# Linear attention gated by a mixer block: scale chains on GpSimd, a fixed turn for the first loads, key-value matrix times WO from rounded parts, and a new order

## The chip, the core and the metric

The kernel runs on one core of one Trainium2 chip. Its engines are TensorE (PE, with its weight loads PEld), VectorE (DVE), ScalarE (ACT), GpSimd (POOL) and SyncE (SP, which here only issues transfers). The metric is device time in microseconds of one execution; lower is better. Times of before: 502.96 us median of 3 runs (502.81, 502.96, 505.84).

## What is computed

x has 2048 rows (tokens) of 512 columns, in fp32. Both branches work on its layer norm; one is linear attention with 32 heads of 16, the other a spatial-shift mixer with an MLP, whose SiLU gates the first.

```python
def _A_ref(x, wqkv, wo):
    # q, k, v from x @ wqkv, 32 heads
    phi = lambda t: jnp.where(t > 0, t + 1, jnp.exp(t)) + 1e-6
    pq, pk = phi(q), phi(k)
    kv = jnp.einsum("bhsd,bhse->bhde", pk, v)
    z = jnp.einsum("bhsd->bhd", pk)
    num = jnp.einsum("bhqd,bhde->bhqe", pq, kv)
    den = jnp.einsum("bhqd,bhd->bhq", pq, z)[..., None] + 1e-6
    return (heads joined of num / den) @ wo

def _B_ref(x, w1, w2, w3, w4):
    h = _gelu(_layernorm(x) @ w1)
    hs = (quarters of h shifted by +1, -1, +2, -2 rows) @ w2
    x1 = x + hs
    return x1 + _gelu(_layernorm(x1) @ w3) @ w4

xn = _layernorm(x)
s = _A_ref(xn, A_wqkv, A_wo)
g = _silu(_B_ref(xn, B_w1, B_w2, B_w3, B_w4))
return x + s * g
```

## The kernel before

The rows are tiled by 128 into 16 tiles, and by four tiles into four blocks (QT = 4). The kernel doesn't issue its instructions where they are written: every helper (`mm`, `act`, `tt`, `ts`, `load`, `store`, `gather` and others) records an operation with what it reads and writes, and `emit` at the end chooses the order of each engine's row. It takes, again and again, the operation that can start first by estimated durations, and among those that can start at about the same time the one with the earliest due time (`op.due`). `deadlines` works the due times out backward from the order in which TensorE's products are written, and `nudged` then shifts single ones by a table of pairs (operation number, steps of a quarter microsecond). That table is SOONER, some 700 pairs. The order is fixed when the program is built; on the chip each engine works through its row and waits on semaphores.

Products of fp32 values are made in one of two ways. `mm(..., slow=True)` multiplies fp32 operands as they are. `products` multiplies values split into a rounded part (fp32r, names ending in h) and a rest (names ending in l): high times high, high times low, low times high, three fp32r products in place of one. `rounded` makes such a pair: ScalarE rounds, VectorE subtracts.

The stages around the change, in the order of time:

- **Start.** SP issues the loads of WK (four chunks wk_s0 to wk_s3, the first in two halves), of block 0 of transposed x (four chunks xt0_0 to xt0_3, each in two halves of 256 columns, since load_u is called with two parts), then of x and WQ. The first products are k0 and k1 from the unrounded first chunks (`raw_k`), then k2 and k3 from the rounded first chunk, then chunk 1 (wk_1h, u0_1h, u0_1l, wk_1l) and so on. At most eight transfers of SP are under way; the ninth waits for the first.
- **Scales.** For each tile the mean and variance of x are taken (`load_rows`). `scale_x` turns them into factors by a chain of small steps on 128 x 1 to 128 x 4 values: w (variance plus epsilon), rs (power of -0.5, on GpSimd), ns (minus rs), nm (mean times ns), mr or a second nm. `spread` makes a similar chain (pu, power, means) whose rows go through memory (arow, nrow) and come back as broadcast rows: `load_u` adds nrow to block b's xt by an accumulating load from GpSimd's queue (`gather`). `mixed` has a chain w2 for the second layer norm. In before, w, ns, pu and w2 stand on VectorE, all other steps on GpSimd.
- **Key-value matrix.** G gathers the product of x and the features of k. Four fp32 products per quarter (kv, with WV) and a mask give kvt, 128 x 512. Its four quarters times the chunks of WO give m, which ScalarE copies into the matrices mq for the attention.
- **Late stages.** Blocks 1 to 3 make the MLP's hidden values first and the down products at the end (`down_forms`, `down_late`), the last of them for block 1, whose hidden values were spilled to memory (hd) and are fetched back.

The lines that the prediction's steps touch are scale_x, spread and mixed (the small steps), the stage of kvt and m, and the call of emit with its table.

Of the kernel before, what the change touches and what calls it, by code (L numbers as in the profile page):

```python
# [11 lines left out]
ALU = mybir.AluOpType  # L12
# [68 lines left out]
class Op:  # L81
    __slots__ = ("eng", "busy", "lat", "emit", "pre", "post", "tiles", "opens", "two", "table", "patience", "soon", "loads",
                 "nom", "due", "ready", "at", "end", "mb", "order")


class Plan:
# [9 lines left out]
    def add(self, eng, busy, lat, reads, writes, emit, two=False, table=None, mb=0.0):  # L96
# [3 lines left out]
        op.order = len(self.ops)  # L100
# [142 lines left out]
    def deadlines(self, first):  # L243
        t = first
        for op in self.ops:
            if op.eng == "PE":
                op.nom = t
                t += op.busy
        for op in self.ops:
            op.due = op.nom if op.eng == "PE" else INF  # L250
        self.backward()
        for op in self.ops:
            op.at = max([p.at + p.lat for p in op.pre], default=0.0)
            if op.eng == "PE":
                op.at = op.nom
            elif any(t.psum for t in op.tiles):
                op.due = min(op.due, op.at + self.PATIENCE)
            elif op.soon:
                op.due = min(op.due, max(op.at, op.soon.at) + op.patience)
            elif op.due == INF and not op.post:  # L260
                op.due = op.at + op.patience
        self.backward()

# [133 lines left out]
def linear_attn_gated_by_mixer(  # L397
# [202 lines left out]
    def scale_x(lo, n):  # L600
# [4 lines left out]
        pl.ts(w, var(mv1, lo, lo + n), kv, EPS, ALU.mult, ALU.add)  # L605
        power(r, w, n)
        pl.ts(s, r, -km if lo < QT else -1.0, None, ALU.mult)
# [8 lines left out]
    def spread(b):  # L616
# [4 lines left out]
        pl.ts(p, var(mv1, b * QT, b * QT + QT), kv * (1.0 + EPS), EPS * EPS, ALU.mult, ALU.add)  # L621
# [401 lines left out]
    def mixed(i, xv):  # L1023
# [11 lines left out]
        pl.ts(w, var(mv2, a, z), KV, EPS, ALU.mult, ALU.add)  # L1035
# [671 lines left out]
    for gg in range(NC):  # L1707
# [4 lines left out]
        pl.tt(kvt.cols(*cs), ps, bmask, ALU.mult)  # L1712
    forms(b)
    mix2(QT + 1)
    for gg in range(NC):
        ps = bank(f"m{gg}")
        pl.mm(ps, kvt.cols(gg * P, (gg + 1) * P), WO.raw[gg], True, True, slow=True)
# [78 lines left out]
    for b in LINE:  # L1796
# [10 lines left out]

    SOONER = (
# [103 lines left out]
```

## Time and profile before

| | us |
|---|---|
| median of 3 runs | 502.96 |
| the profiled execution, its own time | 505.87 |
| span of the profiled execution, first to last instruction | 504.2 |
| TensorE busy | 494.8 |
| VectorE busy | 437.8 |
| ScalarE busy | 373.2 |
| GpSimd busy | 121.2 |

The profile is of one execution. Its lines name an engine, a line of the kernel, an operation and the tiles it writes and reads (out<-in), how often, the busy time, the mean time of one in ns, and how long the engine was idle before it and what ended that idle time. A helper records most operations, so many kinds share one line (L146 is every product, L168 every ScalarE step, L191, L196 and L201 VectorE's and GpSimd's elementwise steps, L225 every accumulating load from GpSimd's queue); the tiles tell them apart. The granted clock is the share of full speed that TensorE was given. TensorE's busy time counts overlapping products once, and the ends of products are modelled, so costs of single products are better read from the distance of their starts.

### The profile page before, as it was taken

How to read it: one execution, taken by the hardware profiler on the slowest of the kernel's cores; microseconds unless marked ns; L12 is line 12 of the kernel's file. 1: busy time of each engine (PE TensorE's matmuls, PEld its weight loads, DVE VectorE, ACT ScalarE, POOL GpSimd, SP SyncE). 2: the span in 40 equal slices, each digit the busy share in tenths (PEclk: the TensorE clock that was granted, in tenths of full speed). 3: DMA queues.
4: the chain of work that ended last, by engine and by line, in shares of the span. 5: the costliest groups of instructions: out<-in, count | busy, mean ns of one | idle time of the engine just before them, and what ended most of it. 6: DMA issues, size and time to landing. Idle time of an engine off the chain costs nothing. (4 is left out here: it accounts for less than half of the span.)

```text
span 504.2 us, 9867 instructions
## 1 busy us (share of the span) xinstructions
PE 494.8 (98%) x3240; PEld 446.5 (89%) x3240; DVE 437.8 (87%) x889; ACT 373.2 (74%) x840; POOL 121.2 (24%) x194
## 2 busy tenths in 40 slices
PE   7999999999999999999999999999999999999896
PEld 4787878888888998899988999999999999999896
DVE  4898997798989958899999999999999799795773
ACT  4798999867687779999988667765766776664631
POOL 1167322447941312133100021100000000234220
PEclk9999999999999999999999999999999999999999
DMA  7949895989995899999987499695444799599995
GB/s 212 317 129 237 231 249 175 210 229 326 316 293 121 228 300 253 278 218 271 347 281 207 148 229 276 185 324 166 136 126 126 216 317 359 128 211 285 296 200 165
DMA packets 87082, 117.44 MB, mean 233 GB/s; under 512 B 10328, under 2 KB 39160, under 8 KB 87032
## 3 DMA queue, kind: packets, MB, share of 16 engines
q1 hardware_dynamic: 75512, 96.11, 58.9%
q0 software_dynamic: 11520, 20.71, 24.8%
q8 instruction: 25, 0.41, 0.3%
q14 instruction: 25, 0.20, 0.1%
HBM read 72.66 MB, written 39.93 MB: 223 GB/s over the span
## 5 line engine op out<-in xcount | busy, mean ns | idle before, releaser
L225 POOL DMA_DIRECT2D xo<-x1d x12 | 11.6, 987 | 158.5 <-ACT d_a121h L168 106.5
L225 POOL DMA_DIRECT2D th<-in_x x14 | 12.1, 885 | 50.0 <-DVE th L201 19.0
L598 POOL TENSOR_TENSOR rs<-w,nhalf 128x4 f32<-128x4 f32 (+2 forms) x10 | 12.4, 1239 | 49.0 <-DVE w L196 35.5
L225 POOL DMA_DIRECT2D o<-xnd x16 | 14.0, 915 | 35.2 <-ACT o L168 15.5
L168 ACT ACTIVATE th<-xo 128x512 f32<-128x512 f32 (+1 forms) x16 | 9.7, 612 | 13.3 <-DVE xo L201 10.8
L225 POOL DMA_DIRECT2D zacc<-ke x12 | 12.0, 1002 | 27.2 <-DMA zacc<-ke 19.7
L225 POOL DMA_DIRECT2D xt<-nrow x16 | 15.2, 1297 | 11.7 <-DMA nrow<-ar 5.8
L191 DVE TENSOR_TENSOR ht<-h,abc 128x512 f32<-128x512 f32 x16 | 11.0, 688 | 5.8 <-PE h L146 5.7
L168 ACT ACTIVATE p<-pe 128x256 f32<-128x256 f32 x20 | 7.6, 382 | 8.0 <-PE pe L146 7.9
L168 ACT ACTIVATE ht<-ht 128x512 f32<-128x512 f32 x16 | 9.8, 624 | 4.1 <-DVE ht L191 4.0
L168 ACT ACTIVATE u<-pb 128x256 f32<-128x256 f32 x20 | 7.6, 381 | 5.9 <-PE pb L146 5.6
L168 ACT ACTIVATE y<-o,nm,rs 128x512 f32<-128x512 f32 x16 | 11.9, 805 | 0.0
L168 ACT ACTIVATE sq<-o,mv 128x512 f32<-128x512 f32 x16 | 11.5, 722 | 0.2
L201 DVE SCALAR_TENSOR_TENSOR pq<-pq,rd 128x512 f32<-128x512 f32 x16 | 10.9, 684 | 0.2
L201 DVE SCALAR_TENSOR_TENSOR qz<-pq,zb 128x512 f32<-128x512 f32 x16 | 10.9, 680 | 0.0
L1456 DVE TENSOR_REDUCE den<-qz 128x32 f32<-128x512 f32 x16 | 10.7, 672 | 0.1
L168 ACT ACTIVATE p<-pb 128x256 f32<-128x256 f32 x20 | 7.6, 382 | 4.2 <-PE pb L146 3.9
L168 ACT ACTIVATE sq<-o 128x512 f32<-128x512 f32 x16 | 10.0, 629 | 0.6 <-PE h L146 0.6
L168 ACT ACTIVATE x<-x,nm,rs 128x512 f32<-128x512 f32 x12 | 9.3, 803 | 0.0
L201 DVE SCALAR_TENSOR_TENSOR th<-th,so 128x512 f32<-128x512 f32 x12 | 8.2, 680 | 0.8 <-ACT th L168 0.7
L168 ACT ACTIVATE sq<-x,mv 128x512 f32<-128x512 f32 x12 | 8.6, 715 | 0.1
L168 ACT ACTIVATE den<-den 128x32 f32<-128x32 f32 x16 | 3.4, 224 | 6.1 <-DVE den L1456 6.0
(2043 smaller groups left out, 2436.2 us busy)
## 6 DMA issues: line engine op xcount, KB each, us to landing
w_s<-in_w SPq DMA_DIRECT2D x28, 256.0 KB, 5.3
x<-in_x SPq DMA_DIRECT2D x16, 256.0 KB, 5.8
xt<-in_xt SPq DMA_DIRECT2D x16, 256.0 KB, 5.1
xnd<-x SPq DMA_DIRECT2D x16, 256.0 KB, 7.0
xt<-nrow POOLq DMA_DIRECT2D x16, 256.0 KB, 7.0
pqd<-qr SPq DMA_DIRECT2D x16, 256.0 KB, 3.2
o<-xnd POOLq DMA_DIRECT2D x16, 256.0 KB, 6.4
x1d<-o SPq DMA_DIRECT2D x16, 256.0 KB
```

Of the source, the lines that this page charges most:

```text
L168: nc.scalar.activation(out.get(), src.get(), func, scale=get(scale), **kw)
L191: self.vec(eng, out, [a, b], lambda: self.e(eng).tensor_tensor(out.get(), a.get(), b.get(), op=op), True)
L201: lambda: self.nc.vector.scalar_tensor_tensor(out.get(), a.get(), get(s), b.get(), op0=op0, op1=op1),
L225: lambda: self.nc.gpsimd.dma_start(out.get(), get(src), accum_op=ALU.add), mb=mb)
L598: lambda: g.tensor_tensor(out.get(), src.get(), nh.get(), op=ALU.pow))
L1456: pl.add("DVE", .6, .68, [t], [den], lambda: nc.vector.tensor_reduce(den.get(), t.get().rearrange("p (h d) -> p h d", d=DH), axis=AX.X, op ...
```

## The change

There are four edits.

- The steps w and ns of `scale_x`, pu of `spread` and w2 of `mixed` go from VectorE to GpSimd.
- `in_turn` gives the first 14 loads of SP a rank, and `deadlines` a due time by the rank, so that they are issued in the order of a list.
- kvt and WO are split into rounded parts and rests, and m is made by `products`.
- The table SOONER is another one, of about the same length.

```diff
@@ deadlines @@
         self.backward()
+        for op in self.ops:
+            if op.rank is not None:
+                op.due = 20.0 * op.rank - 600.0
+
+    def in_turn(self, names):
+
+        ranks = {}
+        for n, name in enumerate(names):
+            ranks.setdefault(name, []).append(n)
+        for op in self.ops:
+            if op.eng == "SP" and op.mb:
+                r = ranks.get(next(iter(op.tiles)).name)
+                if r:
+                    op.rank = r.pop(0)
+
@@ scale_x @@
-        pl.ts(w, var(mv1, lo, lo + n), kv, EPS, ALU.mult, ALU.add)
+        pl.ts(w, var(mv1, lo, lo + n), kv, EPS, ALU.mult, ALU.add, eng="POOL")
         power(r, w, n)
-        pl.ts(s, r, -km if lo < QT else -1.0, None, ALU.mult)
+        pl.ts(s, r, -km if lo < QT else -1.0, None, ALU.mult, eng="POOL")
         pl.tt(m, means(mv1, lo, lo + n), s, ALU.mult, eng="POOL")
@@ spread @@
-        pl.ts(p, var(mv1, b * QT, b * QT + QT), kv * (1.0 + EPS), EPS * EPS, ALU.mult, ALU.add)
+        pl.ts(p, var(mv1, b * QT, b * QT + QT), kv * (1.0 + EPS), EPS * EPS, ALU.mult, ALU.add, eng="POOL")
@@ mixed @@
-        pl.ts(w, var(mv2, a, z), KV, EPS, ALU.mult, ALU.add)
+        pl.ts(w, var(mv2, a, z), KV, EPS, ALU.mult, ALU.add, eng="POOL")
@@ the key-value matrix @@
         pl.tt(kvt.cols(*cs), ps, bmask, ALU.mult)
+    kvr = rounds("kvr")
+    rounded(*kvr, kvt)
+    WO.split()
     forms(b)
     mix2(QT + 1)
     for gg in range(NC):
         ps = bank(f"m{gg}")
-        pl.mm(ps, kvt.cols(gg * P, (gg + 1) * P), WO.raw[gg], True, True, slow=True)
+        products(ps, [both(kvr, gg * P, (gg + 1) * P) + WO.chunk(gg)])
@@ the order @@
+    pl.in_turn(["wk_s0", "xt0_0", "wk_s0", "xt0_0", "wk_s1", "xt0_1", "wk_s2", "xt0_2", "wk_s3", "xt0_3", "x0", "xt0_1",
+                "xt0_2", "xt0_3"])
     SOONER = (
-        15, 75, 17, -32, 23, 4, 27, 4, 31, 4, 39, 3, 45, 46, 47, -6, 48, -56, 62, 6, 81, 2, 106, -37, 110, -38,
...
+        48, -110, 56, 31, 58, 1, 65, 7, 88, -136, 91, -34, 100, 23, 101, 2, 106, -95, 119, 3, 121, -105, 124, 8,
...
```

What the edits make of the engines' rows is seen at three places. First, SP's row at the start; wk_s are the chunks of WK, xt0 those of block 0 of transposed x (a name's last number only tells tiles apart). Before:

```order
L207 DMA wk_s0_100<-in_wqkv 128x256 x2
L207 DMA xt0_0_110<-in_xt 128x256 x2
L207 DMA xt0_1_118<-in_xt 128x256
L207 DMA wk_s1_120<-in_wqkv 128x512
L207 DMA wk_s2_122<-in_wqkv 128x512
L207 DMA xt0_2_124<-in_xt 128x256
L207 DMA wk_s3_126<-in_wqkv 128x512
L207 DMA xt0_3_130<-in_xt 128x256
L207 DMA x0_132<-in_x 128x512
```

And SP's row at the start after the change:

```order
L207 DMA wk_s0_100<-in_wqkv 128x256
L207 DMA xt0_0_106<-in_xt 128x256
L207 DMA wk_s0_100<-in_wqkv 128x256
L207 DMA xt0_0_106<-in_xt 128x256
L207 DMA wk_s1_118<-in_wqkv 128x512
L207 DMA xt0_1_120<-in_xt 128x256
L207 DMA wk_s2_122<-in_wqkv 128x512
L207 DMA xt0_2_124<-in_xt 128x256
L207 DMA wk_s3_128<-in_wqkv 128x512
L207 DMA xt0_3_130<-in_xt 128x256
L207 DMA x0_133<-in_x 128x512
```

The halves of the first two chunks alternate now, and wk_s1 stands ahead of xt0_1 instead of behind it. From wk_s2 to x0 nothing moves.

Second, GpSimd's row around the accumulating loads of block 1 (xt1 from nrow); rs1 from w4 is the power of block 1's scale, an from pu the power for nrow, zacc the sum of k's features. Before:

```order
L598 TENSOR_TENSOR an_98<-pu1_441,nhalf_85 128x4
L598 TENSOR_TENSOR an_98<-pu0_451,nhalf_85 128x4
L225 DMA xt1_0_251<-nrow_318 128x512
L225 DMA xt1_1_264<-nrow_318 128x512
L225 DMA zacc_86<-kr1_381 128x512
L225 DMA xt1_3_284<-nrow_318 128x512
L225 DMA xt1_2_304<-nrow_318 128x512
L598 TENSOR_TENSOR rs1_92<-w4_545,nhalf_85 128x4
L191 TENSOR_TENSOR nm1_95<-mv1_90,ns1_94 128x4
```

The same place in GpSimd's row after the change:

```order
L613 TENSOR_TENSOR an_98<-pu0_401,nhalf_85 128x4
L196 TENSOR_SCALAR pu1_428<-mv1_90 128x4
L613 TENSOR_TENSOR an_98<-pu1_428,nhalf_85 128x4
L225 DMA zacc_86<-kr0_262 128x512
L196 TENSOR_SCALAR an_98<-mv1_90 128x4
L196 TENSOR_SCALAR w4_463<-mv1_90 128x4
L613 TENSOR_TENSOR rs1_92<-w4_463,nhalf_85 128x4
L196 TENSOR_SCALAR ns1_94<-rs1_92 128x4
L191 TENSOR_TENSOR nm1_95<-mv1_90,ns1_94 128x4
L225 DMA xt1_0_252<-nrow_321 128x512
L225 DMA xt1_1_264<-nrow_321 128x512
```

The power for nrow has its first step (pu1) in the same row now, and the whole chain of w4 with the means (an) stands ahead of the loads of xt1 instead of behind them.

Third, TensorE's row at the first of the products m (pbm5 belongs to the mixer's second product). Before, and then after the change:

```order
L146 MATMUL pem5_2522<-w2_t1l_2003,hs11h_2220 128x256
L146 MATMUL pem5_2522<-w2_t1h_1896,hs11l_2308 128x256
L146 MATMUL m0_2555<-wo_s0_2343,kvt_2456 128x512
L146 MATMUL pem5_2522<-w2_b22h_1998,hs41h_2257 128x256
L146 MATMUL pem5_2522<-w2_b22l_2053,hs41h_2257 128x256
```

TensorE's row there after the change:

```order
L146 MATMUL pbm5_2512<-w2_t2l_2063,hs21h_2293 128x256
L146 MATMUL pbm5_2512<-w2_t2h_1956,hs21l_2304 128x256
L146 MATMUL m0_2575<-wo_0h_2403,kvrh_2509 128x512
L146 MATMUL m0_2575<-wo_0l_2413,kvrh_2509 128x512
L146 MATMUL m0_2575<-wo_0h_2403,kvrl_2529 128x512
L146 MATMUL pbm5_2512<-w2_t3h_1943,hs31h_2172 128x256
```

One product of fp32 operands has become three of fp32r operands. Between the last product of kv and m0 stand 30 products of the mixer in the new row.

More of the change, by code (lines that the diff above doesn't have):

```diff
@@ L82 @@
     __slots__ = ("eng", "busy", "lat", "emit", "pre", "post", "tiles", "opens", "two", "table", "patience", "soon", "loads",
-                 "nom", "due", "ready", "at", "end", "mb", "order")
+                 "nom", "due", "ready", "at", "end", "mb", "order", "rank")
 class Plan:
@@ L99, in add @@
         op.pre, op.post, op.tiles, op.opens = {}, [], {}, False
-        op.order = len(self.ops)
+        op.order, op.rank = len(self.ops), None
         op.patience, op.soon = self.patience, False
```

122 rows, old and new, of the table SOONER are left out of this document.

## The prediction, made before the result was known

> **What bounds the kernel now.** I read the page's busy shares first, then the windows of a few stretches, then the waits of PE alone. The windows print time, the busy time of PE, PEld, DVE, ACT and POOL with instruction counts, then the granted clock, the DMA share and GB/s.
>
> ```profile
> PE 494.8 (98%) x3240; PEld 446.5 (89%) x3240; DVE 437.8 (87%) x889; ACT 373.2 (74%) x840; POOL 121.2 (24%) x194
> ...
> 0.00:5.00 5.00, 3.48 (x9) 1.94 (x10) 0.48 (x2) 2.21 (x4) 1.33 (x9) 1.00 0.55 135
> 5.00:10.00 5.00, 3.41 (x13) 2.22 (x14) 2.28 (x6) 1.58 (x4) 0.00 (x0) 1.00 0.84 247
> 10.00:15.00 5.00, 4.67 (x13) 3.39 (x14) 4.99 (x12) 3.97 (x11) 0.94 (x1) 0.66 0.91 279
> ...
> 150.00:200.00 50.00, 50.00 (x310) 43.74 (x309) 42.46 (x94) 40.36 (x96) 11.25 (x16) 1.00 0.82 218
> ...
> 470.00:480.00 10.00, 8.73 (x69) 8.05 (x68) 9.10 (x18) 6.43 (x12) 2.55 (x3) 1.00 1.11 298
> ...
> 490.00:504.20 14.20, 10.13 (x86) 9.92 (x84) 5.73 (x12) 2.07 (x4) 0.86 (x1) 0.95 0.63 167
> ```
>
> TensorE is the bound: 504.2 us of span less 494.8 busy leaves 9.4 us. The first 15 us hold 1.52 + 1.59 + 0.33 = 3.4 of them, the end 4.1, the stretch at 470 1.3. So the kernel gets shorter in three ways only: less TensorE work, a shorter start, fewer waits on the way. The end is a chain of ScalarE, VectorE and a store behind the last matmul, which the change leaves alone. The waits of PE (us in total, times, longest), with the first row of that end from the chain of waits ahead of them:
>
> ```profile
> 500.17 0.39 ACT th L168
> ...
> PE k L146 <- ACT u_1h L168: 1.6, 1, 1.6
> ...
> PE pad L146 <- DVE d_a120l L191: 0.7, 1, 0.7
> PE pb L146 <- DVE h_a221f L191: 0.5, 1, 0.5
> ...
> PE ped L146 <- DVE d_s1xl L191: 0.5, 1, 0.5
> PE k L146 <- DVE wk_1l L191: 0.3, 1, 0.3
> ```
>
> Behind the start only pad, pb and ped wait, 1.7 us together. The largest wait is k's, at the start; the timeline (start, length, idle before) shows what it hangs on:
>
> ```profile
> 2.49 1.92 PE L146 MATMUL k<-zacc,ones 128*128 128x512 f32 x2
> ...
> 7.84 0.40 PE L146 MATMUL k<-wk_0h,u_0l 128*128 128x512 f32 x1
> 8.84 0.63 ACT L168 ACTIVATE wk_1h<-wk_s 128x512 fp32r<-128x512 f32 x1 [3.24 <-DMA wk_s<-in_wqkv]
> ...
> 9.38 0.40 ACT L168 ACTIVATE u_1h<-xt 128x256 fp32r<-128x256 f32 x1
> ...
> 9.83 0.73 PE L146 MATMUL k<-wk_1h,u_1h 128*128 128x512 f32 x2 [1.59 <-ACT u_1h L168]
> ```
>
> ScalarE sits idle until the second chunk of WK lands at 8.84, rounds it, rounds u_1, and PE starts 0.99 us behind the landing. In the next window the clock is 0.66: 0.34 x 5 = 1.7 us of TensorE speed is lost right behind that gap.
>
> **The fixed turn of the loads.** Two swaps count. The first x chunk comes second instead of third, so the first k product can start about when PE goes idle (2.49 + 1.92 = 4.41); but what is gained there ends in the same gap of 1.59 us, so it is worth nothing by itself. The second swap puts wk_s1 ahead of xt0_1 (128 KB). Both are needed before 9.83, and their sum in bytes stays, so whichever is last lands near 8.84 as now; but then it is the piece that needs only 0.40 us of rounding and not 0.63 + 0.40. At 247 GB/s 128 KB take 0.53 us: wk_s1 at 8.31, rounded at 8.94, u_1h at 9.34, PE at 9.39 instead of 9.83: **0.44 us** less. Bounds: 0 if the landing is set by something else than the bytes ahead; 0.59 if wk_s1 comes early enough for u_1h to start at 8.84 itself. A loss has no reason here, since every byte ahead of the gate was ahead of it before. What is late next is wk_1l on VectorE (0.3 us, the last wait above): it hangs on the same two landings and moves with them. From 11.5 us PE has no wait until pb's, so a shift is carried.
>
> **WO from rounded parts.** PE rows around one of the four products of before, and two of the new kind (512 columns, fp32r):
>
> ```profile
> 196.05 0.28 PE L146 MATMUL pbm<-w_t3h,hs31l 128*128 128x256 f32 x1
> 196.17 1.02 PE L146 MATMUL m<-wo_s,kvt 128*128 128x512 f32 x2
> 196.92 0.39 PE L146 MATMUL pbm<-w_t4h,ha221h 128*128 128x256 f32 x1
> 197.15 0.28 PE L146 MATMUL pbm<-w_t4l,ha221h 128*128 128x256 f32 x1
> ...
> 199.08 0.40 PE L146 MATMUL h<-u_0h,w_0l 128*128 128x512 f32 x1
> 199.31 0.39 PE L146 MATMUL h<-u_0h,w_0h 128*128 128x512 f32 x1
> ```
>
> Starts tell the cost, since ends overlap. A narrow product takes 0.12 (196.05 to 196.17). From 196.17 to 197.15 are 0.98, of which one narrow product is 0.12: the fp32 product costs 0.86. Three fp32r products cost 3 x 0.23 = 0.69. Four times 0.17 are **0.68 us** less on the bound engine. For it VectorE and ScalarE get five subtractions and five roundings more:
>
> ```profile
> L191 DVE TENSOR_TENSOR w_al<-w_s,w_ah 128x512 fp32r<-128x512 f32 x5 | 3.4, 682 | 0.0
> ...
> 193.21 0.62 ACT L168 ACTIVATE w_ah<-w_s 128x512 fp32r<-128x512 f32 x1
> ...
> 189.20 0.71 DVE L155 STREAM_TRANSPOSE y_0z<-y 128x512 f32<-128x512 f32 x1 [0.93 <-ACT y L168]
> ...
> L191 DVE TENSOR_TENSOR kvt<-kv,bmask 128x128 f32<-128x128 f32 x4 | 1.1, 269 | 0.3 <-PE kv L146 0.3
> ```
>
> That is 3.4 us on VectorE and 3.1 us on ScalarE; in 150 to 200 they stand idle for 7.5 and 9.6 us, which hides it. One new dependence is real: the first product used to need a quarter of kvt, now all four quarters rounded. By the new order 30 narrow products (3.6 us) stand between the last kv product and m, and two of the wide ones before the rest kvrl is read (0.46). Against them stand one kvt (0.27), one rounding (0.62), two transposes ahead of it in VectorE's row (0.71 each) and the subtraction itself (0.68): 3.0 us. Covered by 1.1 us; if each queue were a microsecond later than I count, PE would wait about that long, once.
>
> **Scale chains on GpSimd.** The small steps first (ns minimum, median, maximum; count; first and last start), then the power and the product on GpSimd, then the place where GpSimd's turn comes nearest to PE:
>
> ```profile
> L196 DVE TENSOR_SCALAR w<-mv x10: 145/160/170, 13.8 to 248.6; 128x4 f32<-128x4 f32 x7, 128x1 f32<-128x1 f32 x2, 128x2 f32<-128x2 f32 x1
> L196 DVE TENSOR_SCALAR ns<-rs x6: 147/164/170, 15.5 to 88.5; 128x4 f32<-128x4 f32 x3, 128x1 f32<-128x1 f32 x2, 128x2 f32<-128x2 f32 x1
> L196 POOL TENSOR_SCALAR nm<-nm x6: 224/384/544, 65.3 to 250.6; 128x4 f32<-128x4 f32 x6
> ...
> L196 POOL TENSOR_SCALAR an<-mv x4: 224/298/752, 24.0 to 82.1; 128x4 f32<-128x4 f32 x4
> L196 DVE TENSOR_SCALAR pu<-mv x4: 157/170/172, 32.1 to 84.9; 128x4 f32<-128x4 f32 x4
> L598 POOL TENSOR_TENSOR rs<-w,nhalf 128x4 f32<-128x4 f32 x7 | 9.4, 1343 | 35.3 <-DVE w L196 21.8 <-ACT u2m L168 10.5 <-ACT u L168 3.0
> L191 POOL TENSOR_TENSOR nm<-mv,ns 128x4 f32<-128x4 f32 x3 | 1.7, 572 | 2.2 <-DVE ns L196 2.2
> ...
> 32.36 2.67 POOL L598 TENSOR_TENSOR an<-pu,nhalf 128x4 f32<-128x4 f32 x2
> 36.72 1.84 POOL L225 DMA_DIRECT2D xt<-nrow  x2 [1.69 <-DMA nrow<-ar]
> ...
> 42.46 0.63 ACT L168 ACTIVATE u_0h<-xt 128x512 fp32r<-128x512 f32 x1 [0.49 <-DMA xt<-nrow]
> ...
> 44.18 0.48 PE L146 MATMUL k<-wk_0h,u_0h 128*128 128x512 f32 x1
> 30.00:40.00 10.00, 10.00 (x46) 7.98 (x45) 9.93 (x22) 9.76 (x21) 6.42 (x9) 1.00 0.60 155
> ```
>
> Twenty small steps (ten w, six ns, four pu) leave VectorE: 20 x 0.16 = 3.2 us off an engine that PE hardly waits for, so nothing at the end. On GpSimd each costs 0.3 to 0.4, some 7 us on an engine busy for 121 of 504. The w step now waits on GpSimd for the variance itself; today its follower waits there for VectorE's w (35.3 us in all), so the queue stands as long as before, and behind it stand the accumulating loads of zacc and xt, for which ScalarE's u_0h waits. New is the turn: the five steps of the second block's scale (0.38 + 1.34 + 0.38 + 0.57, and one for the means) now stand ahead of the xt loads, about 2.7 us. Today that load leaves at 36.72, the moment nrow has landed, after 1.69 us of idle; PE reads the result 1.09 us after it is rounded (43.09 to 44.18). I take 0, because the five steps can run while nrow is on its way (the power for it, the row's stores and the landing take longer than 2.7 us: from 32.36 to 36.72 now). If they cannot, it is a rival below.
>
> [...]
>
> **The new order.** Every engine's row is permuted. The work stays; waits can go or come. What it can gain is bounded by the 1.7 us of pad, pb and ped, what it can lose by about twice that, 3.4 us, if such waits come at other places as well. I take 0 between them, as nothing in the trace tells a sign.
>
> **The sum.** 0.68 + 0.44 = 1.12 us against the profiled execution's 505.87 (span 504.2 and 1.67 around it): 504.75. But the three runs of before are 502.81, 502.96 and 505.84, and the profiled execution is of the long sort, 2.9 us over the median. The only place in its trace of that size is the start, gap 1.59 and clock 1.7. So in the median run the gap may be smaller or absent, and I count half of the 0.44 there: 502.96 - 0.68 - 0.22 = **502.06 us**, call it 502.1.
>
> **The rivals.** *First, the clock stays up.* If the median run still has the slow window and the shorter gap spares it, 1.7 us more go: 500.4. For it: the window follows the gap at once. Against it: 502.96 is probably a run without that loss. [...]
>
> *Second, slower: GpSimd's turn.* If the five steps are held up behind VectorE and the xt loads leave 2.7 us later, u_0h ends at 45.8, PE waits 2.7 - 1.09 = 1.6 us, and if the clock falls behind it as at the start, 1.7 more: 502.1 + 3.3 = 505.4. The same turn stands before the third block's xt loads: twice makes 508.7. It decides at a delay of 1.1 us.
>
> *Third, slower by the new order.* DMA is at 1.11 and VectorE at 9.1 of 10 in 470 to 480, where PE already waits; a permutation that puts one fetch later there adds waits of the size seen, 1.7 to 3.4: 503.8 to 505.5.
>
> *Fourth, the turn of the loads does nothing,* since 1.59 us of idle may come from transfers that lag for other reasons: 502.3, inside the forecast's own range.
>
> **Chances.** Forecast with the fourth, 501.0 to 503.3: 0.56. Clock kept or waits removed, 499.5 to 501.0: 0.16, of which 0.03 go on below 497.9. GpSimd's turn: 0.10, half of it at two places. New waits from the order: 0.18, mostly 503.3 to 506. A measurement tells about 1% (5.0 us) from no change: faster by more than that needs more than half of all idle to go, 0.03; slower by more, 508.0, comes from the doubled rival (0.05) and the order's tail (0.03), 0.08; within 0.89. The range takes the low bounds, 502.96 - 0.68 - 0.59 - 1.7 = 500.0, and on the other side the third rival and one GpSimd delay, 506.0.
>
> **What would show it.** Right: PE's k<-wk_1h,u_1h idles under 1.2 us and starts by about 9.4; m costs about 0.7 us each, with no wait of PE for kvrl or wo's rests; PE busy about 0.7 us lower; VectorE some 16 instructions fewer. Wrong: PE waiting for u_0h at about 44 with xt loads leaving after 39; a wait of PE for kvrl; new waits of PE between 300 and 480. A median under 500 or over 506 would say that the order, which I put at zero, was the larger part.

## The result, and the profile after

| | before | after |
|---|---|---|
| median of the first comparison (6 runs each) | 504.17 | 498.63 |
| lowest and highest of these runs | 502.69, 505.84 | 498.00, 499.65 |
| the profiled execution, its own time | 505.87 | 499.65 |
| its span | 504.2 | 497.9 |

The ratio is 0.9892 with a 95% interval of 0.9866 to 0.9917: 1.1% less. The changed kernel ran twice more beside other kernels, with ratios of 0.9906 [0.9881, 0.9931] and 0.9916 [0.9883, 0.9949]; the median of its 18 runs is 498.70. The forecast was 502.1 with a range from 500.0. The 91 runs of before that came with the experiments have a median of 503.68, so the change is worth 5.0 us by these medians (4.2 to 5.4 by the three ratios), not the 0.9 that I forecast.

First the page's busy times and the windows of after (time, then busy PE, PEld, DVE, ACT and POOL with counts, then granted clock, DMA share, GB/s):

```profile
PE 492.0 (99%) x3244; PEld 446.9 (90%) x3244; DVE 438.2 (88%) x874; ACT 373.9 (75%) x845; POOL 121.5 (24%) x214
...
0.00:5.00 5.00, 3.95 (x10) 2.75 (x11) 0.68 (x2) 2.35 (x5) 1.33 (x9) 1.00 0.51 134
5.00:10.00 5.00, 5.00 (x16) 3.18 (x15) 3.75 (x9) 2.15 (x5) 0.00 (x0) 1.00 0.93 304
10.00:15.00 5.00, 5.00 (x21) 3.59 (x21) 4.07 (x9) 4.52 (x13) 1.68 (x5) 1.00 0.91 285
...
470.00:480.00 10.00, 10.00 (x86) 10.00 (x86) 7.29 (x16) 4.81 (x9) 1.47 (x2) 1.00 1.07 247
```

The slice 5 to 10 us has lost its 1.59 us of idle, the next one its low clock (0.66 before), and 470 to 480 its 1.27 us of idle. The waits of TensorE behind the first products are these two, with k's, pad's, pb's and ped's all gone:

```profile
PE g L146 <- ACT x0h L168: 0.6, 1, 0.6
PE pem L146 <- ACT p5m L168: 0.3, 1, 0.3
```

At the start, the second chunk of WK is rounded at 7.16 instead of 8.84, and its product follows without idle time:

```profile
7.16 0.63 ACT L168 ACTIVATE wk_1h<-wk_s 128x512 fp32r<-128x512 f32 x1 [1.88 <-DMA wk_s<-in_wqkv]
...
8.77 0.62 PE L146 MATMUL k<-wk_1h,u_1h 128*128 128x512 f32 x2
```

### The profile page after: what moved, and what is told of

Read it like the earlier page. It is cut to its first block, busy times and chain, and to the rows that moved or that the text cites. A ratio compares the mean times of both kernels' runs of the same rounds, so it can differ in the third digit from the quotient of the medians.

```text
span 497.9 us, 9898 instructions
## 1 busy us (share of the span) xinstructions
PE 492.0 (99%) x3244; PEld 446.9 (90%) x3244; DVE 438.2 (88%) x874; ACT 373.9 (75%) x845; POOL 121.5 (24%) x214
## 4 chain that ended last, share of the span: by engine, by line
PE 62%; issue 4%; DMA 2%; ACT 1%; POOL 0%; DVE 0%; POOLq 0%; ACTq 0%
PE pb L146 11%; PE pbd L146 9%; PE acc L146 6%; PE pe L146 6%; PE ped L146 5%; PE pbs L146 5%; PE pbm L146 3%; PE pa L146 3%; PE pad L146 3%; PE pes L146 2%; DMA o<-xnd 2%; PE a L146 2%; PE h L146 2%; PE pem L146 2%; PE pas L146 1%
## 5 line engine op out<-in xcount | busy, mean ns | idle before, releaser
L225 POOL DMA_DIRECT2D zacc<-ke x12 | 13.5, 1125 | 28.1 <-DVE u_2l L191 8.7
L196 POOL TENSOR_SCALAR w<-mv 128x4 f32<-128x4 f32 (+2 forms) x10 | 2.7, 269 | 41.2 <-ACT sq L168 40.9
L613 POOL TENSOR_TENSOR rs<-w,nhalf 128x4 f32<-128x4 f32 (+2 forms) x10 | 9.4, 941 | 0.8
```

What stands on the lines that cost most here:

```text
L196: lambda: self.e(eng).tensor_scalar(out.get(), a.get(), get(s1), get(s2), **kw), False,
L225: lambda: self.nc.gpsimd.dma_start(out.get(), get(src), accum_op=ALU.add), mb=mb)
L613: lambda: g.tensor_tensor(out.get(), src.get(), nh.get(), op=ALU.pow))
```

## The experiments

Most of these kernels keep the order of before or after on every engine. For that, `emit` first chooses the whole order as it did, keeps it as a list with each tile's buffer, and only then issues it; the edit acts on the list. "Before" is measured anew in each comparison.

**The turn of the loads alone, in before.** The list of before, with the 14 loads put first in the order of the change:

```diff
+    def edited(self, seq):
+        loads = [op for op in seq if op.eng == "SP" and op.mb]
+        first = []
+        for name in ["wk_s0", "xt0_0", "wk_s0", "xt0_0", "wk_s1", "xt0_1", ...]:
+            first.append(next(op for op in loads if op not in first and next(iter(op.tiles)).name == name))
+        return first + [op for op in seq if op not in first]
```

> Before, its order kept to the last instruction on every engine; only the first 14 loads go in the fixed turn of the change. Theory S (the start): the key weight chunk wk_s1 lands about 1.7 us earlier, as it did in the trace after, the idle of 1.59 us ahead of k<-wk_1h goes, and with it the low clock of the slice 10 to 15 us: 1.6 to 3.1 us less than before, 501.1 to 502.6 against 504.17. Theory L (what I predicted): wk_s1 only half a microsecond earlier, 0.2 to 0.6 us less, 503.6 to 504.0; then the gain is the order's.

Measured: 501.44 (499.60 to 502.42, 12 runs) against 503.84, ratio 0.9952 [0.9934, 0.9970]. Theory S holds, 2.4 us less (interval 1.5 to 3.3). The windows of its start show no idle ahead of wk_1h. Its clock of 1.00 says less, since an unaltered before can have that too (its second profile, below):

```profile
5.00:10.00 5.00, 4.97 (x17) 3.35 (x16) 3.85 (x9) 2.53 (x7) 0.00 (x0) 1.00 0.96 307
10.00:15.00 5.00, 5.00 (x21) 3.65 (x21) 4.38 (x12) 4.39 (x12) 1.01 (x3) 1.00 0.94 289
```

**The old turn in after,** by the same edit with the list of before.

> After, its order kept; only the first 14 loads go in the turn of before. Theory S: the idle ahead of k<-wk_1h and the low clock come back, 498.63 + 1.6 to 3.1 = 500.2 to 501.7; the waits at 470 to 480 us stay gone, so it stays 2.4 us or more under before. Theory L: 498.8 to 499.2. Theory O (the order alone did it, the turn nothing): 498.6.

Measured: 500.31 (499.67 to 501.89, 8 runs), ratio 0.9931 [0.9910, 0.9953]. The wait is back, at the lower edge of theory S; the clock is not low behind it, so the two don't always go together. Timeline row and window of this kernel:

```profile
9.56 0.74 PE L146 MATMUL k<-wk_1h,u_1h 128*128 128x512 f32 x2 [1.36 <-ACT u_1h L168]
...
10.00:15.00 5.00, 4.67 (x19) 3.27 (x18) 4.65 (x10) 3.63 (x11) 1.78 (x2) 1.00 0.90 266
```

**Products in the idle stretch of before.**

```diff
+        at = next(n for n, op in enumerate(seq) if op.eng == "PE" and any(t.name == "wk_1h" for t in op.tiles))
+        # seven products ones x ones into a bank of their own
+        return seq[:at] + [filler] + seq[at:]
```

> Before with seven more products ones x ones (128x128) on TensorE just ahead of the first product with wk_1h, so that the engine is busy in its idle stretch from about 8.2 to 9.8 us; loads and order as before. Theory C (the idle stretch makes the clock fall): the slice 10 to 15 us shows clock 1.00 instead of 0.66, and the time is 1.3 to 1.7 us less, 502.5 to 502.9. Rival (the clock falls for another reason, for example the rate at which the first products come): clock 0.66 as before and the time the same or up to 0.3 us more, 504.2 to 504.5.

Measured: 502.73 (501.83 to 505.21, 12 runs), ratio 0.9994 [0.9973, 1.0014]: no difference that can be told, though the medians lie 1.1 us apart. The clock of the slice was 1.00 in its profile, but two of its runs had a mean clock of 0.996 all the same, at 505.2. As an unaltered before can show 1.00 there too (its second profile, below), this kernel decides nothing.

**The small steps on VectorE, in after.** `ts` takes a second engine name, by which the step is issued while the plan keeps the first:

```diff
-        pl.ts(w, var(mv1, lo, lo + n), kv, EPS, ALU.mult, ALU.add, eng="POOL")
+        pl.ts(w, var(mv1, lo, lo + n), kv, EPS, ALU.mult, ALU.add, eng="POOL", by="DVE")
```

and so for ns, pu and w2.

> After, its order kept; the small steps of the scale chains (w, ns, pu, w2) are issued on VectorE instead of GpSimd, each at the place in the whole order where the plan has it. As predicted (the move to GpSimd is worth nothing): 498.3 to 499.0. Rival (the move is worth something: these steps stand in VectorE's queue behind wide ones, or hold it up): 499.2 to 500.5, with the wait at a product with x0h or at x<-, u<- in the first 60 us.

Measured: 499.91 (499.43 to 500.48, 6 runs), ratio 0.9921 [0.9897, 0.9946]: 1.2 us above after by the medians, 0.8 by the ratios to before (0.9921 against 0.9906), so rather the rival. The wait is at a place that I hadn't named, the transpose ab of an, which holds GpSimd's power of pu. The wait of PE, then the steps of pu on VectorE and, from the list of those who waited for them, GpSimd's power:

```profile
PE ab L151 <- POOL an L196: 1.1, 1, 1.1
...
L196 DVE TENSOR_SCALAR pu<-mv x4: 152/170/170, 27.1 to 82.5; 128x4 f32<-128x4 f32 x4
...
  POOL an L626: 4.6, 3
```

**After once more, and the small steps on GpSimd in before** (with the turn; the same edit the other way round).

> The changed kernel unaltered, beside the others of this call. Its runs come to 498.0 to 499.7 with a clock of 0.998 or more in all. If the turn alone is worth 1.8 to 2.4 us (501.4 for before with the turn), 2.8 us are left for the rest, of which m is 0.7; if the first measurement of after was a lucky one, it comes nearer to 500.4, which would leave m and little else.

> Before in its order, with the turn of the first 14 loads and with the small scale steps (w, ns, pu, w2) issued on GpSimd, each at its old place. Theory N (the move is worth nothing where the order was made for VectorE): as with the turn alone, 501.1 to 501.8. Theory G (GpSimd's free queue brings these steps sooner): 0.5 to 1.3 us less, 500.1 to 500.9. Theory P (they are late behind GpSimd's wide transfers): 0.5 to 1 us more, 502.0 to 502.5.

Measured: after 498.73 (498.24 to 499.76); the other 503.16 (500.45 to 504.68, 12 runs), ratio 0.9981 [0.9957, 1.0004], 1.7 us above the turn alone and above even theory P, though the two ratios' intervals overlap. Its profile has two waits that the profile of the turn alone hasn't:

```profile
PE pad L146 <- DVE d_a120l L191: 1.2, 1, 1.2
...
PE ab L151 <- POOL an L615: 0.8, 1, 0.8
```

Only ab's has to do with these steps; pad's comes and goes in the old order by itself, as the next runs show. So, by one profile each, an order carries these steps on the engine for which it was made, and pays about 1 us at ab on the other.

**One unrounded product for each m, in after.** `products` for m gives way to one fp32 product of the rounded parts, so the products with the rests are left out.

```diff
-        products(ps, [both(kvr, gg * P, (gg + 1) * P) + WO.chunk(gg)])
+        nc.tensor.matmul(ps, kvr[0] as fp32, WO.hl[gg][0] as fp32, start=True, stop=True)
```

> After in its order, but each product m is again one unrounded product, of the rounded part of WO with the rounded part of the key-value matrix; the two products with the rests are left out, the rounding steps stay. Theory M (the products lie on the path that sets the end): 4 x 0.17 = 0.68 us more than after, 499.3. Rival (TensorE has slack later that takes it up): 498.6 to 498.9.

Measured: 499.01 (498.67 to 499.32, 6 runs) against 498.73 for after: 0.28 us, between the two theories and too close to the runs' spread of 1.5 us to tell. The starts in after again show the price of the new kind, 192.43 to 193.12 = 0.69 us:

```profile
192.43 0.39 PE L146 MATMUL m<-wo_0h,kvrh 128*128 128x512 f32 x1
192.66 0.39 PE L146 MATMUL m<-wo_0l,kvrh 128*128 128x512 f32 x1
192.89 0.40 PE L146 MATMUL m<-wo_0h,kvrl 128*128 128x512 f32 x1
193.12 0.34 PE L146 MATMUL pbm<-w_t3h,hs31h 128*128 128x256 f32 x1
```

**Before, profiled again.**

> The kernel before, unaltered, profiled once more. In its 25 runs beside the first experiments a mean clock of 0.996 or less came five times, at 505.1 us, and 20 runs with a higher clock lay from 501.5 to 504.5. Theory S1 (the low clock of the slice 10 to 15 us is a matter of the run, not of the kernel): this profile shows the same idle of 1.59 us ahead of k<-wk_1h, a clock of 1.00 in that slice with four chances in five, and a time near 503.2. Theory S2 (the idle always brings it): clock 0.66 again and 505.

Measured: 504.29, with k's wait at 1.2 us and a clock of 1.00 behind it: S1. That a run without the low clock took 504.29 was new, and its waits say why:

```profile
PE pad L146 <- DVE d_a120l L191: 2.1, 1, 2.1
...
DVE d1f_s40f L191 <- DMA out<-th: 3.9, 1, 3.9
```

VectorE stood idle for 3.9 us ahead of d1f_s40f, until a store of a finished result `out<-th` had landed. d1f_s40f needs nothing of that store but its buffer: in the order of before it gets the buffer in which th of tile 10 lies. In after it gets another one, and VectorE goes on to it without a wait:

```profile
462.07 0.68 DVE L191 TENSOR_TENSOR d1f_s40f<-d1f_s20f,h_ba120f 128x512 f32<-128x512 f32 x1
```

In the first profile of before the same idle time was 2.45 us, put down to "issue", and TensorE's wait 0.7. Over the seven profiles of kernels with the old order and this buffer (two name the store, five say "issue", so for these the store is inferred), TensorE's wait follows VectorE's:

| idle of VectorE ahead of d1f_s40f, us | 0.8 | 1.3 | 1.6 | 2.5 | 3.0 | 3.6 | 3.9 |
|---|---|---|---|---|---|---|---|
| wait of pad for d_a120l, us | 0 | 0 | 0 | 0.7 | 1.2 | 1.8 | 2.1 |

TensorE's wait is VectorE's less 1.8 us in the last four of them: VectorE has that much slack there, and what goes beyond it TensorE pays.

**That one tile in another buffer, in before,** alone and with the turn. The buffer ab0 has been free since the early blocks.

```diff
+                    if t.name == "d1f_s40f":
+                        pool, tag = self.pools["ab"], "ab0"
```

> Before, order and loads kept; one tile, d1f_s40f, is put into a buffer that has been free for long, instead of the one that th held until its store to out had landed. In two profiles of before VectorE stood idle 2.45 and 3.86 us ahead of d1f_s40f and TensorE 0.66 and 2.07 us ahead of a product with d_a120l. Theory B (the store's landing, which differs from run to run, is what the old order loses between 460 and 480 us): no idle of over 0.5 us ahead of d1f_s40f, the wait of pad for d_a120l gone, 0.7 to 2.1 us less than before, about 502.4 against 503.7, and a smaller spread. Rival (the next wait, such as ped for d_s1xl, grows by as much): 503.7.

> Before with two of its parts replaced: the fixed turn of the first 14 loads, and d1f_s40f in the free buffer; order, products and engines as before. Theory B with theory S: both gains add, 503.7 - 2.3 - 1.3 = 500.1, with a spread of about 1 us, and after is then 1.4 us further, of which m is 0.3 to 0.7. Rival (the turn already took this wait away, since its profile shows none): 501.4, as the turn alone.

Measured: the buffer alone 501.18 (500.37 to 503.45, 12 runs) against 503.69, ratio 0.9964 [0.9946, 0.9982]; with the turn 500.60 (499.19 to 501.79, 9 runs), ratio 0.9943 [0.9924, 0.9962]. Theory B for the buffer alone: 2.5 us by the medians and 1.8 by the ratio (interval 0.9 to 2.7, so the 1.3 us that I had taken from the profiles isn't excluded). The two gains don't add up on this chip: with the buffer in place the turn brings only 0.6 us more by the medians, against 2.4 alone on another chip. Why, no run here shows. In the profile of the buffer alone, its fastest run, wk_1h starts at 7.76 in the old turn, and TensorE waits no more than 0.3 us for that chunk. The stretch 460 to 480 of the first kernel has no idle left (its row in before again below it):

```profile
460.00:480.00 20.00, 20.00 (x170) 20.00 (x170) 16.86 (x34) 12.75 (x25) 4.82 (x6) 1.00 1.09 277
```

```profile
460.00:480.00 20.00, 17.34 (x141) 16.68 (x140) 13.81 (x28) 10.48 (x20) 5.26 (x7) 1.00 1.00 254
```

**Which swap of the turn counts.**

> Before; of the turn only the swap of the first xt0_1 with wk_s1, so that wk_s1 is fifth in the queue; wk_s0 and xt0_0 still go two and two. If the place in the queue decides, wk_1h starts about 0.5 us earlier than in before (8.84 to 8.9 us), near 8.3. If the whole of the gain hangs on it, near 7.2, as after.

> Before; of the turn only the alternation of the halves of wk_s0 and xt0_0; xt0_1 still goes ahead of wk_s1. If the place of wk_s1 decides, wk_1h starts at 8.8 to 8.9 us as before and the first products with the halves some 0.2 us earlier; if the gain hangs on the alternation, wk_1h starts near 7.2.

Measured, one profiled run each: wk_1h started at 7.63 with the swap of wk_s1 and xt0_1 (the run took 503.19), and at 7.92 with the alternation (500.88). The five profiles with the old turn have it between 7.76 and 8.95, the thirteen with the whole turn between 6.65 and 7.16 us. Neither half gives the whole, and one run can't tell either from the best of the old.

**The wait put back into after.** From d1f_s40f on, two buffers change places, for later tiles too:

```diff
+        swapped = {59: 66, 66: 59}   # 66 is th10's
+                    if seen:         # from d1f_s40f on
+                        t.slot = swapped.get(t.slot, t.slot)
```

> After, its order kept; from d1f_s40f on, two buffers change places, so that d1f_s40f stands again behind the landing of a store out<-th (of th10), as in before. Theory B: VectorE idles several us ahead of d1f_s40f, TensorE waits again between 462 and 475 us, and the median rises by 0.7 to 3 us, to 499.4 to 501.7. Rival (the old order lost its time elsewhere and this wait is only where it shows): 498.7, as after.

Measured: 503.91 (502.86 to 506.05, 12 runs), ratio to before 1.0015 [0.9992, 1.0038]. The swap takes back the whole gain of the change, more than theory B had asked for. Among VectorE's waits from 455 to 482 us the one ahead of d1f_s40f is the only one on a transfer. Its waits, VectorE's and TensorE's, and then the windows behind them:

```profile
DVE d1f_s40f L191 <- DMA out<-th: 3.9, 1, 3.9
...
PE pbd L146 <- DVE p1d L191: 2.4, 1, 2.4
...
PE ped L146 <- ACT d_s11h L168: 0.7, 1, 0.7
```

```profile
468.00:470.00 2.00, 0.50 (x2) 0.30 (x2) 1.90 (x5) 2.00 (x6) 0.01 (x1) 1.00 1.14 283
470.00:472.00 2.00, 0.44 (x3) 0.44 (x4) 2.00 (x4) 2.00 (x6) 1.04 (x2) 1.00 0.82 243
472.00:474.00 2.00, 2.00 (x15) 2.00 (x14) 2.00 (x5) 0.87 (x2) 1.57 (x2) 0.70 1.04 152
474.00:476.00 2.00, 2.00 (x11) 2.00 (x11) 1.22 (x3) 0.00 (x0) 0.00 (x0) 0.50 0.92 166
476.00:478.00 2.00, 2.00 (x18) 2.00 (x17) 1.07 (x3) 0.43 (x1) 0.00 (x0) 0.94 0.88 210
```

3.06 us of idle between 468 and 472, and then the clock at one half for 1.2 + 2.0 + 0.24 = 3.4 us, estimated from the slices' 0.70, 0.50 and 0.94 as if it were always 1.00 or 0.50: 1.7 us more. Together that is 4.8 us, where the medians lie 5.2 apart. The low clock didn't come in every run: one of the 12 had a mean clock of 1.000 and still took 502.86.

**What is left of the order.** Three more profiles of before with turn and buffer, then the same kernel timed beside after on one chip.

> Before with the turn and the free buffer, profiled a second time, since its runs lie from 499.2 to 501.8 and its first profile was that of the fastest. Theory W (the old order has other waits, which come and go): a run above 500.3 shows a wait of 0.5 us or more that after has not. Theory R (only transfers at the start differ): the difference lies in the first 20 us, with less than 18.5 us of PE busy.

> The same kernel, profiled a third time, with the same two theories: W a wait of 0.5 us or more after the first 20 us in a run above 500.3; R the difference in the first 20 us.

> The same kernel, profiled a fourth time, with the same two theories: W a wait of 0.5 us or more after the first 20 us in a run above 500.3; R the difference in the first 20 us.

> Before with the turn and the free buffer, timed again beside after on one chip. Theory A (turn and buffer are the whole of what the order and the loads bring; m is the rest): 0.3 to 0.8 us above after. Theory W (the old order has still other waits): 1.5 to 2 us above after, as 500.6 against 498.7 in runs on different chips.

> The changed kernel unaltered, as the other side of that comparison: 498.2 to 499.2 by the two medians so far (498.63, 498.73).

Measured: 499.68, 498.99 and 499.69 in the profiled runs, with no wait behind the first 20 us in any; none was above 500.3, so they put neither W nor R to the test. On one chip 499.52 (499.04 to 499.65, 7 runs) for before with turn and buffer, 498.83 (498.00 to 499.40, 6 runs) for after, 503.56 for before. The difference of 0.69 us is theory A. It is as large as m's term, but no run takes m alone out of it. The 500.6 of the first comparison remains unexplained; it was on another chip.

## Why the prediction was wrong

On one chip the 4.73 us from 503.56 to 498.83 part into 4.04 for the turn and the one buffer together and 0.69 for the rest. By my own steps:

**m, 0.68 forecast: the price was right, its effect on the time is open.** The three products take 0.69 us where one took 0.86, TensorE waits neither for kvrl nor for the rests of WO, and the last comparison leaves 0.69 for m and all else together. The one direct test gave only 0.28, though in its trace the one product takes 0.86 again (starts at 193.50 and 194.36).

**The fixed turn, 0.44 and half of it: mis-sized, 2.4 alone in before and about 1.7 in after.** The mechanism was the one named (wk_s1 earlier, the gap ahead of wk_1h). Two steps failed. I priced the earlier landing as 128 KB at 247 GB/s, 0.53 us, and held that the last landing of the two stays. In after the rate in the slice was 304 GB/s and wk_1h started 1.68 us sooner. That isn't this pair of runs alone: in all thirteen profiles with the whole turn wk_1h starts sooner than in all five with the old one, by 1.6 us from median to median (6.99 and 8.57). Nor is it the rate alone, which ran from 284 to 317 GB/s with the whole turn and from 247 to 299 with the old. Why the swap is worth more than its bytes, no run here shows. And I halved the term since the median run "may" have a smaller gap; the second profile of before, at 504.29, still had 1.2 us of it. A gap of 1.2 to 1.6 us and some 0.3 of clock (below) are still less than the 2.4 measured in before; the rest of it stays open.

**The scale chains, 0: no cost shows in sum, for a reason that I didn't have.** The rival of GpSimd's turn didn't come true; after has no wait near 44 us, and GpSimd's busy time hardly moved (121.2 to 121.5) where I had 7 us more. VectorE's row did matter, though: in the new order the steps on VectorE cost about 1 us at ab, in the old order TensorE has no wait there. That the rival's five steps would be held up behind VectorE was my assumption; what sets the time of a step on GpSimd, no run here shows. In after's trace one w step takes 0.19 us while VectorE works on qi, and another 0.42 while VectorE works on x8l, ending just behind it (83.74 against 83.69). The ten w steps last 0.27 us on average, the longest 0.43, and TensorE has no wait from 30 to 90 us, where these two stand.

```profile
31.31 1.40 DVE L201 SCALAR_TENSOR_TENSOR qi<-q,rs,cq 128x512 f32<-128x512 f32 x2
31.55 0.19 POOL L196 TENSOR_SCALAR w<-mv 128x4 f32<-128x4 f32 x1
...
83.01 0.68 DVE L191 TENSOR_TENSOR x8l<-x,x8h 128x512 fp32r<-128x512 f32 x1
83.32 0.42 POOL L196 TENSOR_SCALAR w<-mv 128x4 f32<-128x4 f32 x1
...
L196 POOL TENSOR_SCALAR w<-mv 128x4 f32<-128x4 f32 (+2 forms) x10 | 2.7, 269 | 41.2 <-ACT sq L168 40.9
```

**The new order, 0: the step that failed most.** I wrote that what it can gain is bounded by the 1.7 us of pad, pb and ped, as one profile showed them. The profile had the cause in it, in the waits of VectorE, a row that I didn't follow:

```profile
DVE d1f_s40f L191 <- issue: 2.5, 1, 2.5
```

This wait, for a landing, differs from run to run: it showed 0 to 2.1 us on TensorE in seven profiles. In the timed runs the buffer alone is worth 1.8 us (ratio) to 2.5 (medians) in before. Swapped back into after it costs 5.2, where TensorE idled for 3.1 us in the profiled run and the clock fell behind it. The sentence that a median under 500 would mean that the order was the larger part was half right: alone, turn and buffer weigh about the same, and together they bring less (3.1 on one chip, 4.0 on another) than the sum of the two.

**The clock rival, 0.16 with the waits removed: it came true, at a fifth of its price.** The time lies below its band all the same: my bands left 497.9 to 499.5 without a chance, and 498.6 fell there. Of the 91 runs of before, 19 had a mean clock of 0.996 or less, with a median of 504.99; the other 72 had 503.33. The 73 runs of kernels with the new turn all had 0.998 or more (the one with the wait put back into after left out). So the low clock of the profile that I read was a one in five event, 1.7 us in that run and about 0.3 on average. That also undoes my base: 502.96, from three runs, was 0.7 under the median of 91, and the two sorts of run that I saw in it are a spread from 500.5 to 506.8.

**The chance of 0.03 for more than 1%** asked for more than half of all idle to go. Between the two profiles idle fell by only 3.5 us (9.4 to 5.9), but 1.7 us of low clock and 0.7 of m came on top of it, 5.9 of the 6.3 us between the two spans.

## What to carry to other kernels

A buffer that is freed by a store's landing can be a wait on a transfer, even for a tile that has nothing to do with it (here 3.9 us ahead of d1f_s40f, for out<-th): where a planner hands out buffers by estimated landings, give the ones behind stores to those who can wait, and follow any idle ahead of a first write to a tile, also where it's put down to "issue". One profile shows one draw of a wait on a transfer (here 0.8 to 3.9 us on VectorE in seven), so bound a term by several, or by the size of the idle behind it. And the worth of a wait isn't its length alone where the clock falls behind it (here 3.1 us of idle and 1.7 us of clock).

## What was not expected of the hardware

The clock fell to one half for nearly the same time at two places: 3.4 us after the idle at 468 to 472 above, and in the first profile of before after 1.92 us of idle spread over 8 to 11:

```profile
8.00:9.00 1.00, 0.24 (x2) 0.00 (x0) 0.16 (x1) 0.16 (x1) 0.00 (x0) 1.00 0.93 281
9.00:10.00 1.00, 0.17 (x1) 0.17 (x2) 0.72 (x2) 1.00 (x3) 0.00 (x0) 1.00 1.03 378
10.00:11.00 1.00, 0.67 (x3) 0.24 (x4) 1.00 (x3) 1.00 (x3) 0.00 (x0) 1.00 1.00 355
11.00:12.00 1.00, 1.00 (x4) 0.79 (x5) 1.00 (x3) 0.91 (x3) 0.00 (x0) 0.70 1.00 266
12.00:13.00 1.00, 1.00 (x4) 0.81 (x3) 1.00 (x4) 0.97 (x4) 0.00 (x0) 0.50 0.84 221
13.00:14.00 1.00, 1.00 (x3) 0.76 (x3) 1.00 (x4) 1.00 (x5) 0.00 (x0) 0.50 0.85 244
14.00:15.00 1.00, 1.00 (x4) 0.79 (x3) 0.98 (x3) 0.10 (x1) 0.94 (x1) 0.59 0.85 307
```

By the same estimate that is 0.6 + 1 + 1 + 0.82 = 3.4 us again. An idle of 2.1 us in one piece (before again, at pad) and one of 1.4 us (after with the old turn) left it at 1.00. The longest idle without a product between was 2.40 us at the first place and 1.59 us at the second. Why the one idle stretch costs the clock and the other doesn't, no run here shows.
